# Gated linear attention with two feed-forward layers on one core: the second attention product in four column groups, and the second layer's weights prepared in two slots of three

## The chip, the core and the metric

The kernel runs on one core of a Trainium2 chip. The metric is the device time of one execution in microseconds. The core has a matrix engine (PE, with its weight loads shown apart as PEld), three elementwise engines (DVE, ACT, POOL) and a queue engine (SP) that issues most DMAs. They run side by side and wait for one another through semaphores.

## What is computed

A gated recurrence (an mLSTM cell) over 768 steps, 4 batches and 8 heads of width 40, and then two feed-forward layers over the 3072 tokens of width 320, each with 2048 hidden channels. All of it is in float32:

```
for t in range(S):
    m_new = max(f[t] + m, i[t]);  f_s = exp(f[t] + m - m_new);  i_s = exp(i[t] - m_new);  m = m_new
    C = f_s * C + i_s * outer(v[t], k[t]);   n = f_s * n + i_s * k[t]
    y[t] = sigmoid(o[t]) * (C @ q[t]) / max(|n . q[t]|, 1)
x = y as (3072, 320)
x = (h * clip(h + 3, 0, 6) / 6) @ w1_out     with h = x @ w1_in
x = (max(h, 0) ** 2) @ w2_out                with h = x @ w2_in
```

## The kernel before

**Attention.** The recurrence is cut into 12 chunks of 64 steps. A unit `u` is one chunk of one batch (48 units), all 8 heads together. For a unit, `at_S` (lines 355 to 382) makes the scores, `at_P` multiplies them with the decay weights `W` into the tile `Xm` (104 partitions, for each head 104 columns: 64 for the outputs of the chunk's steps, 40 for the next state), and **`at_Y`** (lines 398 to 408) makes the second product. For each head it multiplies `Xm`, as the stationary operand, with `Z` (104 partitions, 41 columns: the chunk's values, a column of ones, and the carried state). The first 64 columns of `Xm` give 64 rows of output at partitions 0 to 63 (line 404), the other 40 give the next state at partitions 64 to 103 (line 406). The output is 64 and 40 columns of the array, so the two products of a head sit in two column groups of it. Afterwards `at_C` copies the state into the next `Z`, and `at_n1` to `at_n3` normalise and gate the output.

A float32 product is one instruction in the program and two records in the trace, each a weight load and a matmul. So a unit's `at_Y` is 16 instructions, 16 records on line 404 and 16 on line 406.

**Feed-forward layers.** They are cut into slots `s` (200 of them; layer 1 is slots 0 to 103, layer 2 slots 104 to 199). A full slot has the first product of 128 hidden channels for 512 tokens (`mm_A`, line 551, 8 matmuls of 512 columns), the activation on ACT and DVE (`act1` line 560 or 562, `act1b` line 567 or 570), the split of the result into a high and a low part (`act2` line 575 on ACT, `act2b` line 580 on DVE), and two slots later the second product (`mm_B`, line 590, 12 matmuls of 320 columns). Every fp32 operand of the layers is taken apart into a high part in the faster fp32r format and a remainder. `t_pe`, `t_hi` and `t_lo` (lines 525 to 539) transpose and split the layer's input.

**Weights.** Each layer has 16 weight tiles, `wi` (first product, even `i`) and `wo` (second product, odd `i`). They arrive as 64-bit words. `w_load` fetches a tile, `w_exp` (line 486, ACT) mends the exponent, `w_b1` and `w_b2` (lines 492 and 498, DVE) put the float32 together in the tile `wt`, `w_hi` (line 507, ACT) and `w_lo` (line 512, POOL) make the two parts. Tile `i` of layer 2 stands in the place of tile `i` of layer 1. The tile `wi` with index `i` is first used by `mm_A` of slot 104 + i, `wo` with index `i` by the `mm_B` that runs in slot 105 + i.

**Order.** The first part of the program (to about 196 us) follows a list written out by hand, `FIRST`. From there on the order comes from the function `moe`: for each slot `mm_A`, `act1`, `act1b`, then the steps hooked to the slot's "pe" place, then `mm_B` of two slots ago, the steps hooked to its "ew" place, `act2` and `act2b`. A unit's `at_Y` is hooked to every second slot (`2 * u - 10`), `at_S` of the next unit right after it in the same slot. The steps on layer 2's weights are hooked from slot `s1 = 90` on.

Of the kernel before, what the change touches and what calls it, by code (L numbers as in the profile page):

```python
# [25 lines left out]
L = 64  # L26
# [78 lines left out]
def kernel(ctx, tc, qk, kn, va, gates, og, w1i, w1o, w2i, w2o, out):  # L105
    nc = tc.nc
# [7 lines left out]
    E0 = 64  # L114
    KX = E0 + D
# [32 lines left out]
    Z = [[const.tile([KX, H, DV], F32, name=f"Z{b}{i}") for i in range(2)] for b in range(B)]  # L148
# [249 lines left out]
    def at_Y(u):  # L398
        b, c = units[u]
        Xm = T["X", u]  # L400
        pool, tag = (ps_acc, "acc0") if u in (1, 3) else (ps_y, "y")
        Yp = pool.tile([KX, H, DV], F32, tag=tag, name="Yp")
        for h in range(H):
            nc.tensor.matmul(  # L404
                out=Yp[0:L, h, :], lhsT=Xm[:, h, 0:L], rhs=Z[b][c % 2][:, h, :], start=True, stop=True)
            nc.tensor.matmul(  # L406
                out=Yp[E0:KX, h, :], lhsT=Xm[:, h, L:KX], rhs=Z[b][c % 2][:, h, :], start=True, stop=True)
        T["Y", u] = Yp

    def at_C(u):  # L410
# [216 lines left out]
    w_bits = (w_b1, w_b2)  # L627
    w_hilo = (w_hi, w_lo)
# [11 lines left out]
    def at(s, part, f, *a):  # L640
        hooks.setdefault((s, part), []).append((f, *a))
# [31 lines left out]
    for u in range(6, NU):  # L673
        b, c = units[u]
        if c % 2:
            at(at_slot[u] + 3, "pe", x_T, 0, c // 2, b)
    for u in range(UL, NU):
        s = at_slot[u]
        if u >= 6:
            at(max(s - 6, 0), "ew", at_load, u)  # L680
            at(max(s - 6, 0), "ew", at_gload, u)
        if u >= 5:
            at(max(s - 4, 0), "ew", at_weights, u)
            at(max(s - 3, 0), "ew", at_x2, u)
        if u >= US:
            at(s - 3, "ew", qk_split, u)
        at(max(s - 2, 0), "pe", at_S, u)
        at(max(s - 2, 0), "ew", at_P, u)
        at(s, "pe", at_Y, u)
        at(s, "ew", at_C, u)  # L690
        at(s, "ew", at_norm, u)
    for j in range(NB):
        for i in range(B):
            at(first[1, j, 0] - 13 + 3 * i, "pe", x_T, 1, j, i)
    s1 = first[0, NB - 1, 0] + 2
    for i in range(NS):
        at(s1 + i, "ew", w_load, 1, i)
        at(s1 + i + 3, "ew", w_exp, 1, i)
        at(s1 + i + 4, "ew", w_bits, 1, i)
        at(s1 + i + 5, "ew", w_hilo, 1, i)  # L700
    for p, s in ((4, 45), (5, 45)):
        at(s - 6, "ew", o_load, p)
        at(s, "ew", o_sig, p)
# [3 lines left out]
        o_load, load_gates, o_sig, at_load, const_init, gate_m, gate_g, gate_G, gate_b,  # L707
        gate_bT, at_gload, w_load, w_add, w_mask, w_e, x_q, at_S, at_P, w_exp, x_k,
        w_b1, w_b2, at_Y, at_n1, at_n2, at_n3, at_C, w_hi, w_lo, warm, t_pe, t_hi,
        t_lo, mm_A, act1, act1b, act2, act2b, mm_B, evac)}  # L710
    todo = []
# [65 lines left out]
```

## Time and profile before

| | us |
|---|---|
| median of 3 runs | 871.29 (871.28 to 873.6) |
| the profiled execution | 871.86 |
| span of its instructions | 870.1 |
| PE busy in the span | 825.9 (95%) |
| DVE / ACT / POOL busy | 559.5 / 427.4 / 260.7 |

Read it in stretches, for the limits differ. Matmuls are pipelined and their ends are modelled, so the starts of records say more than their durations. A record with `x8` is a run of eight that follow each other; its first start is shown. The granted PE clock is full (2.4 GHz) from 119 us on; before that it falls to half in three short stretches.

### The profile page before, as it was taken

What the parts mean: (1) busy time and instruction counts of PE and PEld (TensorE: products, weight loads), DVE (VectorE), ACT (ScalarE), POOL (GpSimd) and SP (SyncE); (2) the same over time, 40 slices, a digit from 0 to 9 for tenths busy, and PEclk for the clock granted to TensorE, in tenths of its full rate; (3) what the DMA queues carried; (4) which work ended last, traced back from release to release, by engine and by line L of the source; (5) the groups of instructions that cost most, each with busy time, mean ns of one, the idle gap of its engine ahead of it and who ended that gap; (6) DMA issues with size and microseconds to landing.
All of it is one profiled execution on the core that took longest, in us unless ns stands there. A gap on an engine that the chain in (4) does not pass through costs nothing.

```text
span 870.1 us, 15963 instructions
## 1 busy us (share of the span) xinstructions
PE 825.9 (95%) x6288; PEld 738.0 (85%) x6288; DVE 559.5 (64%) x938; ACT 427.4 (49%) x817; POOL 260.7 (30%) x240
## 2 busy tenths in 40 slices
PE   3597999999999999999999999999999999999998
PEld 2486887888888888888889988999999999999997
DVE  4879889777878877777644999444444344444332
ACT  4656665645557455554434765343343433433433
POOL 4857865354454544545100444000000000000000
PEclk9999889999999999999999999999999999999999
DMA  8974521343633434333004540000000000000000
GB/s 222 269 232 134 169 81 36 92 100 96 170 92 97 103 86 108 95 81 82 1 3 167 201 163 1 1 31 1 1 31 1 20 12 1 31 1 1 31 1 31
DMA packets 30694, 66.82 MB, mean 77 GB/s; under 512 B 5116, under 2 KB 17468, under 8 KB 30620
## 3 DMA queue, kind: packets, MB, share of 16 engines
q1 hardware_dynamic: 30620, 65.82, 26.5%
q8 instruction: 49, 0.80, 0.4%
q14 instruction: 25, 0.20, 0.1%
HBM read 61.77 MB, written 4.03 MB: 76 GB/s over the span
## 4 chain that ended last, share of the span: by engine, by line
PE 73%; DVE 16%; issue 5%; ACT 3%; POOL 1%; DMA 1%; SPq 0%; DVEq 0%; POOLq 0%; ACTq 0%
PE hps L551 33%; PE acc L590 32%; DVE wt L492 4%; DVE gl L580 3%; PE Yp L404 3%; PE Sp L372 2%; DVE g L567 2%; PE tp L525 2%; DVE wt L498 1%; DVE X L444 1%; ACT yt L431 1%; ACT g L560 1%; DVE gh L575 1%; DVE Xm L395 1%; PE Sp L379 1%
## 5 line engine op out<-in xcount | busy, mean ns | idle before, releaser
L551 PE MATMUL hps<-xs,wi 128*128 128x512 f32 (+1 forms) x1600 | 392.6, 389 | 4.2 <-DVE g L567 2.4
L590 PE MATMUL acc<-wo,gh 128*128 128x320 f32 x1536 | 349.5, 314 | 0.3 <-ACT X L597 0.3
L551 PEld LDWEIGHTS hps<-xs,wi 128*128 128x128 f32 x1600 | 290.5, 193 | 53.5 <-DVE g L567 2.7
L590 PEld LDWEIGHTS acc<-wo,gh 128*128 128x128 f32 x1536 | 259.6, 189 | 9.9 <-ACT X L597 0.5
L590 PE MATMUL acc<-wo,gl 128*128 128x320 f32 x768 | 239.3, 312 | 5.0 <-DVE gl L580 5.0
L580 DVE TENSOR_TENSOR gl<-g,gh 128x512 fp32r<-128x512 f32 (+1 forms) x200 | 154.2, 771 | 61.7 <-ACT gh L575 60.6
L575 ACT CAST gh<-g 128x512 fp32r<-128x512 f32 (+1 forms) x192 | 115.1, 600 | 75.3 <-DVE g L570 58.7
L570 DVE TENSOR_TENSOR g<-g 128x512 f32<-128x512 f32 x96 | 66.4, 692 | 133.2 <-ACT g L562 133.2
L590 PEld LDWEIGHTS acc<-wo,gl 128*128 128x128 f32 x768 | 144.9, 189 | 7.6 <-DVE gl L580 7.5
L560 ACT ACTIVATE g<-hps,three 128x512 f32<-128x512 f32 (+1 forms) x104 | 67.8, 655 | 152.0 <-PE hps L551 138.4
L562 ACT ACTIVATE g<-hps 128x512 f32<-128x512 f32 x96 | 57.3, 597 | 143.4 <-PE hps L551 143.4
L567 DVE SCALAR_TENSOR_TENSOR g<-g,hps 128x512 f32<-128x512 f32 (+1 forms) x104 | 66.8, 644 | 65.0 <-ACT g L560 64.5
L329 POOL TENSOR_TENSOR Xm<-qkt,W 40x512 f32<-40x512 f32 x36 | 49.8, 1384 | 119.2 <-ACT W L319 113.6
L404 PEld LDWEIGHTS Yp<-Z,Xm 104*64 104x64 f32 x768 | 54.5, 151 | 21.8 <-issue 13.3
L404 PE MATMUL Yp<-Z,Xm 104*64 104x41 f32 x768 | 60.6, 244 | 8.8 <-DVE Xm L388 3.8
L300 POOL TENSOR_TENSOR W<-W,bT 104x512 f32<-104x512 f32 x43 | 59.4, 1382 | 3.4 <-DMA W<-Gd 3.0
L406 PE MATMUL Yp<-Z,Xm 104*40 104x41 f32 x768 | 52.7, 225 | 0.3 <-POOL Xm L340 0.3
L512 POOL TENSOR_TENSOR wi<-wt,wi 128x768 fp32r<-128x768 f32 x14 | 27.6, 1970 | 83.7 <-ACT wi L507 83.5
L340 POOL TENSOR_TENSOR Xm<-kI,W 104x320 f32<-104x320 f32 x43 | 40.5, 944 | 25.2 <-DMA Z<-in_va 10.4
L406 PEld LDWEIGHTS Yp<-Z,Xm 104*40 104x40 f32 x768 | 46.5, 123 | 0.4 <-POOL Xm L340 0.4
L351 DVE SCALAR_TENSOR_TENSOR qs<-qs,less,qkt 120x512 fp32r<-120x512 f32 x52 | 37.6, 764 | 7.5 <-ACT qs L349 7.3
L306 POOL TENSOR_SCALAR_AFFINE_SELECT W<-W 64x512 f32<-64x512 f32 x48 | 36.7, 767 | 9.7 <-DVE W L300 6.8
(90 smaller groups left out, 664.2 us busy)
## 6 DMA issues: line engine op xcount, KB each, us to landing
qkt<-in_qk SPq DMA_DIRECT2D x74, 160.0 KB
W<-Gd SPq DMA_DIRECT2D x48, 208.0 KB
rwi<-in_w1i SPq DMA_DIRECT2D x8, 768.0 KB
rwi<-in_w2i SPq DMA_DIRECT2D x8, 768.0 KB
rwo<-in_w1o SPq DMA_DIRECT2D x8, 640.0 KB
rwo<-in_w2o SPq DMA_DIRECT2D x8, 640.0 KB
Z<-in_va SPq DMA_DIRECT2D x48, 82.0 KB
X<-in_og SPq DMA_DIRECT2D x6, 640.0 KB
```

The costliest lines, as they stand in the source:

```text
L300: on("w_add", "g", u).tensor_tensor(out=W, in0=W, in1=bT[:, c, b * H:(b + 1) * H].unsqueeze(2).to_broadcast([KX, H, L]), op=ALU.add)
L329: on("x_q", "g", u).tensor_tensor(out=x_tile(u)[E0:KX, :, 0:L], in0=T["qk", u][E0:KX, 0], in1=T["W", u][E0:KX], op=ALU.mult)
L404: nc.tensor.matmul(out=Yp[0:L, h, :], lhsT=Xm[:, h, 0:L], rhs=Z[b][c % 2][:, h, :], start=True, stop=True)
L406: nc.tensor.matmul(out=Yp[E0:KX, h, :], lhsT=Xm[:, h, L:KX], rhs=Z[b][c % 2][:, h, :], start=True, stop=True)
L551: nc.tensor.matmul(out=h, lhsT=w[:, hl, kk, o:o + P], rhs=t[:, xk, i0 * P:i1 * P], start=(i == 0), stop=(i == len(TERMS) - 1))
L560: nc.scalar.activation(out=g, in_=T["h", s], func=ACTF.Relu, bias=three)
L562: nc.scalar.activation(out=g, in_=T["h", s], func=ACTF.Relu)
L567: nc.vector.scalar_tensor_tensor(out=g, in0=g, scalar=6.0, in1=T["h", s], op0=ALU.min, op1=ALU.mult)
L570: nc.vector.tensor_tensor(out=g, in0=g, in1=g, op=ALU.mult)
L575: copy("act2", s)(out=gh, in_=g)
L580: nc.vector.tensor_tensor(out=gl, in0=g, in1=gh.bitcast(F32), op=ALU.subtract)
L590: nc.tensor.matmul(out=acc[i], lhsT=g[:, n], rhs=w[:, hl, m % MG, :], start=(m == 0 and q == 0), stop=(m == NM - 1 and q == 2))
```

## The change

Two things. In `at_Y` each head's 104 columns of `Xm` are cut at 32, 64 and 96, so that four products (32, 32, 32 and 8 columns) stand where two (64 and 40) stood. The operands `Z`, the outputs and the waits are the same; a unit has 32 instructions and 64 records where it had 16 and 32. And the steps on layer 2's weights, one tile in every slot, are spread: `3 * i // 2` takes the place of `i`, so two tiles are treated in three slots. The loads keep their slots.

```diff
         for h in range(H):
-            nc.tensor.matmul(
-                out=Yp[0:L, h, :], lhsT=Xm[:, h, 0:L], rhs=Z[b][c % 2][:, h, :], start=True, stop=True)
-            nc.tensor.matmul(
-                out=Yp[E0:KX, h, :], lhsT=Xm[:, h, L:KX], rhs=Z[b][c % 2][:, h, :], start=True, stop=True)
+            for o in range(0, KX, 32):
+                e = min(o + 32, KX)
+                nc.tensor.matmul(
+                    out=Yp[o:e, h, :], lhsT=Xm[:, h, o:e], rhs=Z[b][c % 2][:, h, :],
+                    start=True, stop=True)
...
     for i in range(NS):
         at(s1 + i, "ew", w_load, 1, i)
-        at(s1 + i + 3, "ew", w_exp, 1, i)
-        at(s1 + i + 4, "ew", w_bits, 1, i)
-        at(s1 + i + 5, "ew", w_hilo, 1, i)
+        s = s1 + 3 + 3 * i // 2
+        at(s, "ew", w_exp, 1, i)
+        at(s + 1, "ew", w_bits, 1, i)
+        at(s + 2, "ew", w_hilo, 1, i)
```

The order of PE's instructions around the last unit's `at_Y`. `Yp` is the output, `Xm` and `Z` the operands, the shape is columns of `Xm` by columns of `Z`. Before:

```order
L551 MATMUL hps<-xs,wi_1421 128x512 x8
L404 MATMUL Yp<-Z_108,Xm 64x41
L406 MATMUL Yp<-Z_108,Xm 40x41
L404 MATMUL Yp<-Z_108,Xm 64x41
L406 MATMUL Yp<-Z_108,Xm 40x41
```

Now (line 406 is the one matmul of the new loop):

```order
L552 MATMUL hps<-xs,wi_1613 128x512 x8
L406 MATMUL Yp<-Z_108,Xm 32x41 x3
L406 MATMUL Yp<-Z_108,Xm 8x41
L406 MATMUL Yp<-Z_108,Xm 32x41 x3
L406 MATMUL Yp<-Z_108,Xm 8x41
```

Nothing else moved on PE: each head has four instructions in a row where it had two.

The order of DVE's instructions early in layer 2, where `wt` is the weight being put together, `g` and `gl` are the slot's activation and its low part. Before:

```order
L492 TENSOR_SCALAR wt<-rwi_6093 128x768
L498 SCALAR_TENSOR_TENSOR wt<-rwi_6093,wt 128x768
L580 TENSOR_TENSOR gl<-g,gh 128x512
L570 TENSOR_TENSOR g<-g 128x512
L492 TENSOR_SCALAR wt<-rwo_6130 128x640
L498 SCALAR_TENSOR_TENSOR wt<-rwo_6130,wt 128x640
L580 TENSOR_TENSOR gl<-g,gh 128x512
L570 TENSOR_TENSOR g<-g 128x512
L492 TENSOR_SCALAR wt<-rwi_6167 128x768
L498 SCALAR_TENSOR_TENSOR wt<-rwi_6167,wt 128x768
```

Now (the same steps have line numbers one higher):

```order
L493 TENSOR_SCALAR wt<-rwo_6736 128x640
L499 SCALAR_TENSOR_TENSOR wt<-rwo_6736,wt 128x640
L581 TENSOR_TENSOR gl<-g,gh 128x512
L571 TENSOR_TENSOR g<-g 128x512
L581 TENSOR_TENSOR gl<-g,gh 128x512
L571 TENSOR_TENSOR g<-g 128x512
L493 TENSOR_SCALAR wt<-rwi_6772 128x768
L499 SCALAR_TENSOR_TENSOR wt<-rwi_6772,wt 128x768
```

One slot in three now has no weight between its `g` and its `gl`.

## Rows read from the trace of the kernel before

**Rows 1.** Stretches: us, busy (count) of PE, PEld, DVE, ACT, POOL, clock, DMA.

```profile
0.00:118.00 118.00, 81.99 (x997) 72.74 (x998) 92.21 (x156) 71.04 (x179) 80.73 (x88) 0.93 0.66 194
...
196.00:440.00 244.00, 243.42 (x2185) 215.38 (x2184) 188.19 (x348) 128.87 (x211) 109.54 (x99) 1.00 0.36 90
...
515.00:540.00 25.00, 24.27 (x132) 20.81 (x132) 24.67 (x29) 16.53 (x30) 11.77 (x7) 1.00 0.08 27
```

**Rows 2.** The chain that ended last, shares by line, 196 to 440 us.

```profile
by line: PE hps L551 38.4%; PE acc L590 37.1%; PE Yp L404 9.4%; PE Sp L372 6.0%; PE tp L525 2.0%; PE Yp L406 1.4%; issue 1.2%; DVE qs L351 0.9%; ACT X L451 0.8%; DVE gl L580 0.6%; ACT L451 0.5%; ACT qs L349 0.4%; DVE g L567 0.4%; DVE Xm L39
```

**Rows 3.** The same chain from 138 to 197 us.

```profile
by line: PE acc L590 25.6%; PE hps L551 20.7%; DVE gl L580 9.0%; PE Yp L404 6.3%; DVE gh L575 5.5%; issue 5.2%; ACT g L560 4.5%; PE Sp L379 4.3%; DVE g L567 3.4%; ACT L319 2.2%; DVE Xm L395 2.2%; ACT X L451 2.0%; ACT W L319 2.0%; ACT X L597
```

**Rows 4.** Timeline of PE's matmuls in one slot: start, us, line, operation, shapes.

```profile
297.19 2.00 PE L551 MATMUL hps<-xs,wi 128*128 128x512 f32 x8
299.12 0.25 PE L404 MATMUL Yp<-Z,Xm 104*64 104x41 f32 x1
299.12 0.27 PE L406 MATMUL Yp<-Z,Xm 104*40 104x41 f32 x2
...
299.23 0.20 PE L406 MATMUL Yp<-Z,Xm 104*40 104x41 f32 x1
...
299.27 0.24 PE L406 MATMUL Yp<-Z,Xm 104*40 104x41 f32 x2
...
299.35 0.20 PE L406 MATMUL Yp<-Z,Xm 104*40 104x41 f32 x1
...
299.38 0.23 PE L406 MATMUL Yp<-Z,Xm 104*40 104x41 f32 x1
...
299.90 0.21 PE L406 MATMUL Yp<-Z,Xm 104*40 104x41 f32 x1
299.95 0.29 PE L404 MATMUL Yp<-Z,Xm 104*64 104x41 f32 x2
300.17 0.65 PE L372 MATMUL Sp<-qs 120*64 120x64 f32 x8
```

**Rows 5.** Line 404 from 196 to 440 us: count, ns min/median/max, first and last start.

```profile
L404 PE MATMUL Yp<-Z,Xm x432: 230/230/251, 198.1 to 436.3; 104*64 104x41 f32 x144
```

**Rows 6.** Timeline of PE at a block that started with an empty queue.

```profile
141.88 0.68 PE L379 MATMUL Sp<-qkt 40*64 40x64 f32 x16 [0.45 <-issue]
```

**Rows 7.** Line 404 from 141.7 to 142.3 us: the semaphore wait ahead of its block.

```profile
L404 PEldq EVENT_SEMAPHORE  x1: 51/51/51, 142.0 to 142.0; - x1
```

**Rows 8.** Timeline of PE: first products of slots without attention (85, 86, 87).

```profile
438.36 2.00 PE L551 MATMUL hps<-xs,wi 128*128 128x512 f32 x8
...
442.29 2.00 PE L551 MATMUL hps<-xs,wi 128*128 128x512 f32 x8
445.89 2.00 PE L551 MATMUL hps<-xs,wi 128*128 128x512 f32 x8
```

**Rows 9.** Timeline of PE: first products of slots 106 and 112.

```profile
515.86 2.00 PE L551 MATMUL hps<-xs,wi 128*128 128x512 f32 x8
...
540.20 2.00 PE L551 MATMUL hps<-xs,wi 128*128 128x512 f32 x8
```

**Rows 10.** Waits of PE's loads, 505 to 545 us: total us, times, longest.

```profile
PEld acc L590 <- DVE gl L580: 1.9, 5, 0.5
```

**Rows 11.** Groups by line, 505 to 545 us: count, busy us, mean ns, idle before.

```profile
L580 DVE TENSOR_TENSOR gl<-g,gh 128x512 fp32r<-128x512 f32 x12 | 8.7, 728 | 1.4 <-ACT gh L575 1.4
L512 POOL TENSOR_TENSOR wi<-wt,wi 128x768 fp32r<-128x768 f32 x4 | 7.8, 1945 | 9.4 <-ACT wi L507 9.4
L492 DVE TENSOR_SCALAR wt<-rwo 128x640 int32<-128x640 int32 x4 | 7.7, 1935 | 0.0
...
L570 DVE TENSOR_TENSOR g<-g 128x512 f32<-128x512 f32 x9 | 6.2, 685 | 0.0
...
L498 DVE SCALAR_TENSOR_TENSOR wt<-rwi,wt 128x768 int32<-128x768 int32 x4 | 3.8, 960 | 0.1
...
L536 DVE TENSOR_TENSOR xs<-tp,xs 128x256 fp32r<-128x256 f32 x2 | 0.8, 422 | 0.0
```

## The prediction

> **What bounds the kernel now.** I read the stretches first. From 196 to 440 us PE is busy for 243.4 of 244 us at the full clock, while DVE has 188 and POOL 110 [rows 1]: whatever PE is spared there comes off the end, as long as nothing else fills up. Before 118 us PE has 82 of 118 us, DVE 92, POOL 81: a mixture of waits, where a shorter PE block is mostly swallowed. From 515 to 540 us it is the other way round, DVE is busy for 24.67 of 25 us and PE waits. After that PE is gapless to the end. The chain of waits says the same: from 196 to 440 us it lies on PE, and lines 404 and 406, the second attention product, have 10.8% of it, 26 us [rows 2].
>
> Next the block itself [rows 4]. Read starts, not durations. The first product's last matmul starts shortly before 299, the block starts at 299.12 and the next block (line 372) at 300.17: 1.05 us, of which the 16 records of line 404 take 299.12 to 300.01, a record every 58 to 59 ns. Line 406 starts at the same 299.12, so the two column groups work at the same time. In its first records it goes faster: from 299.23 to 299.38, over 299.27, 299.31 and 299.35, four steps of 38 ns. Then it is held back to the pace of line 404 and ends at 299.90, only some 0.1 us ahead of it. So two things can be seen: a 64-column record costs 58 ns and a 40-column record 38 ns with the same 41 moving columns; and a later instruction may overtake waiting ones of the other group, but only by a few records, since line 406 never gets further ahead than that.
>
> **The second product in four groups.** It removes nothing of the arithmetic; it cuts the 64-column record, the slow one, into two of 32. Per group there are still 16 records one after the other (8 heads, two records each). At 58 ns these take 16 x 0.058 = 0.93 us; at the 38 ns of the 40-column records 16 x 0.038 = 0.61 us. 32 and 8 columns are fewer than 40, but the 41 moving columns are still there, so I take no less than 38 ns. The most that a unit can gain is thus 0.93 - 0.61 = 0.32 us.
>
> From this comes off what four groups need and two did not. First, overtaking: for the fourth group's record to start beside the first, it must pass one waiting record of each of the three other groups, three records, about as far as line 406 ran ahead of line 404. That is just enough for all four to run, with some loss; I charge 5 to 10% of 0.61 us, 0.05 us. Second, feeding: 32 instructions must reach the array in 0.6 us. The nearest row is a block that began with an empty queue [rows 6]: its eight float32 products started at 141.88, and PE's sequencer was at the wait that stands behind all eight by 142.0 [rows 7]. The rounding leaves 0.1 to 0.2 us, at most 25 ns an instruction, 0.8 us for 32 in the worst case and some 0.5 us in the best; but during the 1.9 us of matmuls of 512 columns ahead of the block the queue has time to fill, so part of the 32 is there at the start. I charge 0.02 us. The result is a gain of 0.25 us a unit, between 0.10 (groups half in step) and 0.32.
>
> How often does it count? Line 404 has 432 records from 196 to 440 us, 16 a unit, 27 units [rows 5]: 27 x 0.25 = 6.8 us (2.7 to 8.6). What is late next there is POOL, then DVE: 110 and 188 us of 244, which is no bound at 237 either. Of the 21 units before, the chain from 138 to 197 us has 6.3% of 59 us on line 404, 3.7 us, four units [rows 3]; between them it runs over DVE and ACT, so I count 0.8 us of their 1.0. Ahead of 138 us I count nothing, and 0.5 us of either sign for the order in which waits end there and for the half-clock stretches of that part.
>
> The trace shows a record every 29 ns over both groups (32 in 0.92 us). The Trainium skill (page "TensorEngine Tiling", section Instruction Overhead) speaks against the change: a matmul costs about 60 cycles however few columns it moves, so one should not take the tiling factor from a dimension that is already small. At the granted 2.4 GHz that is 25 ns; if it held for the whole array, 64 records would take an estimated 1.6 us, 0.7 us more than now. The two records that start together at 299.12 agree with it at most within one group.
>
> **The weights in two slots of three.** A slot without attention takes 442.29 to 445.89, 3.60 us, and 3.93 us (438.36 to 442.29) where the layer's input is transposed [rows 8]. The six slots 106 to 111 take 515.86 to 540.20, 24.34 us [rows 9]; two of them transpose, so they should take 4 x 3.60 + 2 x 3.93 = 22.26. The loss is 2.1 us, and PE's own waits agree: 1.9 us in five waits for `gl`, DVE's line 580 [rows 10]. The cause is DVE's sum. A slot with a weight has 0.73 (line 580) + 0.69 (line 570) + 1.94 (line 492) + about 0.9 (line 498) = 4.2 us [rows 11] against 3.60 on PE; the excess adds up from slot to slot until the two slots of lag are used up.
>
> Now three slots hold two weights: 3 x 1.42 + 2 x 2.84 = 9.9 us, and 0.8 us at most for a transposed block (two subtractions of up to 0.42 [rows 11]), 10.7, against 2 x 3.60 + 3.93 = 11.1 on PE. DVE falls behind by 0.6 us in the first weighted slot and, where that one is followed by a weight and a transpose, by 1.7 us in all, and catches up in the slot without a weight. Before, the excess of about 0.6 us a slot had to run for many slots before PE felt it, so I take the whole 2.1 us as gained (1.6 to 2.2). PE's matmuls after it follow without a gap, so it reaches the end.
>
> What the spread costs is time to the deadline. The last `wi` (index 14) has its DVE steps in slot 115 and its split in slot 116, and slot 118 needs it. ACT and POOL take 0.8 and 1.95 us for the split (POOL's piece is line 512 [rows 11], ACT's is the shorter one), so it is there at about the middle of slot 117, some 1.9 us early. The last `wo` (index 15), split in slot 117, is needed in slot 120. If that cover were gone it would cost one wait of up to 2 us, once. The steps are only moved later past other work on ACT and POOL, which have room there: 16.5 and 11.8 of 25 us [rows 1]. The loads keep their place on the queue.
>
> **Sum.** 871.86 (the profiled execution) - 6.8 - 0.8 - 2.1 = 862.2; it lies 0.57 above the median of the runs, so against that 871.3 - 9.7 = **861.6**.
>
> **Rivals.**
> A. The forecast: all four groups run together.
> B. Overtaking stops short: three groups run, the fourth waits for most of its records, and each unit gains at most 0.1 us. For it: line 406 was held back after a few records [rows 4]. Against it: three records ahead is just what is needed. Time: 871.3 - 2.1 - (0 to 2.7) - 0.3 = 866 to 869, say 867.5.
> C. The moving columns share one path. Four groups read the same 41 columns of `Z` four times. Line 551 moves 8 x 512 columns in at most 1.93 us (297.19 to 299.12), 2.1 columns per ns; the block at 141.88 moves 16 x 64 in 0.68 us less the last record's tail of some 0.2, 2.2 per ns [rows 4, 6]. I see no higher rate. Two groups of 41 stay below it, four would need 164 columns in 38 ns, twice that. If 2.2 is the limit, a round of four records takes 75 ns, a block 16 x 0.075 = 1.19 us, 0.27 us more than now: 27 x 0.27 = 7.3, less 2.1, so **876.5**. It decides as soon as a round takes over 58 ns. Against it: nothing in the rows shows the path full with small matmuls, the loads of 64 columns set the same pace in that block. The Trainium skill's page "TensorE: Matmul & The Clock Gate" (Measured speedup against the span model) has three column groups of 512 moving columns 2.38 times as fast as one, which no run here shows.
> D. A price per record for the whole array, whatever its group. The densest stretch is 23 to 29 ns a record [rows 4]. 64 records at 25 to 29 ns take 1.6 to 1.86 us, 0.7 to 0.9 more: 27 x 0.8 = 22, less 2.1, so about 891. Against it: the pairs at 299.12, and that line 404 goes on at 58 ns whether or not line 406 runs beside it.
>
> **Chances.** A 0.66, B 0.15, C 0.12, D 0.07. The spread of the weights gains its 2 us in all four. A change under 0.3% (2.6 us) is about what a measurement of this kernel cannot tell from none. A is faster; of B a little more than half; C and D are slower. Faster 0.75, same 0.06, slower 0.19. The range covers A to its ends (27 x 0.32 = 8.6, with 1.3 before 196 us, 2.2 and 0.5: 858.7) and B to its upper end, 869.3, and leaves C and D out.
>
> **What would show it.** In the new trace the block of the second product (from 196 to 440 us) should take 0.8 us to the next block instead of 1.05, with records of the four groups starting within some 20 ns of each other and a record per group every 38 to 43 ns; slots with attention should be 0.25 us shorter and the others as they were. Slots 106 to 111 should be 3.60 and 3.93 us long, without a wait of line 590 for `gl`. A round of 75 ns speaks for C; starts spaced evenly by 25 ns for D; one group trailing the other three for B. The forecast is wrong if the blocks get no shorter, or if DVE or POOL take over the stretch from 196 to 440 us.

## The result, and the profile after

| | median, us | range, runs | ratio to the kernel before | 95% interval |
|---|---|---|---|---|
| before | 872.44 | 871.28 to 874.01, 4 | | |
| changed | 860.34 | 858.38 to 861.24, 4 | 0.9857 | 0.9829 to 0.9885 |
| changed, once more (e10) | 860.09 | 857.02 to 862.32, 5 | 0.9863 | 0.9841 to 0.9884 |

The change saves 11.6 to 12.1 us; 9.7 were forecast. The profiled execution of the changed kernel is the fastest of its first four (858.38 us, span 856.6), so the two traces differ by 13.5 us, more than the medians.

Stretches of the changed kernel, to be read against [rows 1] (us, busy and count of PE, PEld, DVE, ACT, POOL, clock, DMA):

```profile
0.00:118.00 118.00, 77.11 (x1434) 67.74 (x1434) 94.51 (x157) 71.54 (x181) 82.55 (x88) 0.94 0.66 194
196.00:440.00 244.00, 241.83 (x3027) 213.19 (x3026) 185.96 (x351) 130.82 (x214) 109.91 (x98) 1.00 0.34 88
515.00:540.00 25.00, 25.00 (x143) 22.54 (x142) 20.05 (x28) 15.61 (x26) 9.09 (x5) 1.00 0.00 1
```

PE is no longer quite full from 196 to 440 us (2.2 us free where it had 0.6), DVE and POOL are where they were, and from 515 to 540 us PE is full and DVE has 5 us to spare where it had 0.3. The chain of waits in the second stretch has 6.0% on the second product where it had 10.8 [rows 2], and small shares for `qs` that were not there in that size:

```profile
by line: PE hps L552 35.4%; PE acc L591 34.4%; PE Yp L406 6.0%; PE Sp L372 5.3%; issue 2.9%; PE tp L526 2.2%; DVE qs L351 2.2%; ACT qs L349 2.1%; DMA Z<-in_va 1.4%; ACT X L598 1.3%; DMA kI<-in_kn 1.0%; ACT g L561 0.8%; ACT X L452 0.8%; SPq 
```

One slot, the timeline of PE's matmuls (start, us, line, operation, shapes) beside [rows 4]. The second line is an answer for the first 80 ns of the block alone:

```profile
290.33 2.00 PE L552 MATMUL hps<-xs,wi 128*128 128x512 f32 x8
...
292.26 0.28 PE L406 MATMUL Yp<-Z,Xm 104*32 104x41 f32 x8
...
292.26 0.80 PE L406 MATMUL Yp<-Z,Xm 104*32 104x41 f32 x64
292.99 0.65 PE L372 MATMUL Sp<-qs 120*64 120x64 f32 x8
```

From the block's start to the next block it is 0.73 us; it was 1.05. Eight records, two of each group, have started within 80 ns: all four groups run together. The group of all records in this block gives first and last start, 292.3 and 292.9. In finer figures of the same trace the four groups start 7 ns apart, a round of four takes 38 ns, and the last record starts 0.605 us after the first.

Where the 13.5 us of this pair of traces lie is read from the starts of slots. Slots 32, 85, 106 and 112 after:

```profile
191.91 2.00 PE L552 MATMUL hps<-xs,wi 128*128 128x512 f32 x8
...
426.99 2.01 PE L552 MATMUL hps<-xs,wi 128*128 128x512 f32 x8
...
504.49 2.00 PE L552 MATMUL hps<-xs,wi 128*128 128x512 f32 x8
...
526.73 2.00 PE L552 MATMUL hps<-xs,wi 128*128 128x512 f32 x8
```

Before, slot 32 started here (for the others see [rows 8, 9]; slot 85 is 438.36):

```profile
196.14 2.00 PE L551 MATMUL hps<-xs,wi 128*128 128x512 f32 x8
```

So 4.23 us were gained ahead of slot 32, 7.14 in slots 32 to 84, nothing up to slot 106, 2.10 in slots 106 to 111, and nothing more to the end (870.1 - 856.6 = 13.5). From slot 32 on all of these repeat to within 0.25 us in every trace below that has that part of the change (e8 changes slots 42 to 74 further); the first does not.

### The profile page after: what moved, and what is told of

The parts are those of the page before. It is cut to its first block, busy times and chain, and to the rows that moved or that the text cites. A ratio compares the mean times of both kernels' runs of the same rounds, so it can differ in the third digit from the quotient of the medians.

```text
span 856.6 us, 19035 instructions
## 1 busy us (share of the span) xinstructions
PE 804.5 (94%) x7824; PEld 717.7 (84%) x7824; DVE 549.3 (64%) x938; ACT 427.2 (50%) x817; POOL 263.2 (31%) x240
## 4 chain that ended last, share of the span: by engine, by line
PE 78%; DVE 9%; issue 4%; ACT 4%; POOL 3%; DMA 1%; SPq 1%; POOLq 0%; ACTq 0%; DVEq 0%
PE hps L552 37%; PE acc L591 35%; PE Yp L406 2%; DVE gl L581 2%; PE tp L526 2%; PE Sp L372 2%; DVE wt L499 1%; DVE g L568 1%; DVE wt L493 1%; ACT g L561 1%; POOL Xm L329 1%; DVE qs L351 1%; ACT qs L349 1%; DVE X L445 1%; POOL W L306 1%
## 5 line engine op out<-in xcount | busy, mean ns | idle before, releaser
L406 PEld LDWEIGHTS Yp<-Z,Xm 104*32 104x32 f32 (+1 forms) x3072 | 35.9, 111 | 26.6 <-issue 16.8
L406 PE MATMUL Yp<-Z,Xm 104*32 104x41 f32 (+1 forms) x3072 | 42.5, 211 | 13.6 <-issue 5.8
L445 DVE TENSOR_TENSOR X<-X,yt 64x320 f32<-64x320 f32 x34 | 31.7, 932 | 1.1
L513 POOL TENSOR_TENSOR wo<-wt,wo 128x640 fp32r<-128x640 f32 x16 | 26.6, 1664 | 18.5 <-ACT wo L508 18.4
```

The costliest lines, as they stand in the source:

```text
L406: nc.tensor.matmul(out=Yp[o:e, h, :], lhsT=Xm[:, h, o:e], rhs=Z[b][c % 2][:, h, :], start=True, stop=True)
L513: on("w_lo", "g", ph, i).tensor_tensor(out=w[:, 1], in0=f, in1=w[:, 0].bitcast(F32), op=ALU.subtract)
```

## The experiments

**One part alone.** In e1 only the weights' steps are spread, in e2 only the groups are cut. In e3 the whole change is made, but units 0 to 20 keep two groups, in e11 only those units have four and nothing else is changed. e9, e10 and e12 are kernels that were there already (before, changed, e1), run again.

```
e3:   for o, e in CUT4 if u >= 21 else CUT2:
e11:  for o, e in CUT4 if u < 21 else CUT2:      (weights as before)
      CUT2 = ((0, 64), (64, 104))
      CUT4 = ((0, 32), (32, 64), (64, 96), (96, 104))
```

> The kernel before with only the spread of the weights. Theory: the whole 2.1 us lies in slots 106 to 111, which go from 24.34 to 22.2 us (3.60, or 3.93 with a transpose), everything else stays, so the time falls by 2.1 us, ratio 0.9976. Rival (the deadline): the later tiles make PE wait once or twice between slots 112 and 120, and less than 1 us is left. Rival (the two edits feed each other): alone it gains clearly less or more than 2.1 us.

> The kernel before with only the four column groups. Theory: blocks of 0.73 us instead of 1.06 to the next block, so 23 of the 27 units from slot 32 on gain 0.32 us, three gain nothing and one loses 0.3 us (7.1 us), and the part before 196 us gains some 3 us: about 10 us, ratio 0.9885. The weights' loss in slots 106 to 111 stays at 2.1 us. If the part before 196 us gains only what was forecast (0.8 us), 7.9 us, ratio 0.991.

> The changed kernel, but units 0 to 20 keep two column groups; so up to about 186 us the program is the one of before. Theory 1 (shorter blocks of the first units gain some 3 us): this kernel lacks them and is 3 us slower than the changed one, 9.2 us faster than before, ratio 0.9895. Theory 2 (the gain before 196 us is scatter of the half-clock stretches, nothing to do with the blocks): as fast as the changed kernel, ratio 0.986.

| | median, us | beside it before | ratio | 95% interval |
|---|---|---|---|---|
| e1, weights | 868.35 | 872.25 | 0.9948 | 0.9931 to 0.9966 |
| e2, groups | 863.06 | 872.25 | 0.9892 | 0.9874 to 0.9909 |
| e3, groups from unit 21 on, weights | 859.93 | 872.25 | 0.9870 | 0.9850 to 0.9890 |

e2 gained 9.2 us, between the 10 of its theory and the 7.9 of the alternative, with 7.07 of them between slots 32 and 85 in its trace. The other two did not fit shorter blocks in the first units: e1 gained 3.9 us where its trace has 2.10 in slots 106 to 111, and e3 was as fast as the whole change (its theory 2) though it has two groups in the first part. Both said that the first 196 us scatter, or that something else shortens them. Four more kernels, with twelve runs of three of them, were made for that:

> The kernel before, unchanged, in the place of a changed kernel. In the kernel with the spread weights alone the time fell by 3.9 us, 1.8 more than the trace shows in slots 106 to 111, though its first 196 us are instruction for instruction those of before. Theory 1 (the runs that stand for the kernel before have a slower first part by their place in the series): this one is some 1.5 to 2 us faster than the kernel before, ratio 0.998. Theory 2 (scatter from run to run, or something in how a program lies on the chip): ratio 1.000 within its interval.

> The changed kernel, unchanged, beside the kernel before on the same chip. Steady part and weights by the traces: 7.07 + 2.10 = 9.2 us. Theory 1 (four groups gain nothing before 196 us): 9.2 us less than the kernel before in the same place of the series. Theory 2 (they gain some 3 us there): 12 us less than it.

> The kernel before with four column groups in units 0 to 20 alone; from slot 32 on and in the weights it is the kernel before. Theory 1 (the shorter blocks of the first units give the changed kernel its extra 2 to 3 us before 196 us): 2 to 3 us faster than before, ratio 0.997. Theory 2 (they give the forecast 0.8 us or nothing, and the rest comes from elsewhere): 0 to 0.8 us, ratio 0.999 to 1.000, as the first part of the kernels with two groups there scatters.

> The kernel with the spread weights alone once more, since it gained 3.9 us where its trace shows 2.1 in slots 106 to 111 and the first 440 us are those of before. Theory 1 (the first part really runs some 2 us shorter in this program, with the same instructions there): 3.9 us again, ratio 0.9955. Theory 2 (the first part scatters by several us from run to run, and six runs were luck): 2.1 us, ratio 0.9976.

| | median, us | beside it before | ratio | 95% interval |
|---|---|---|---|---|
| e9, before again | 872.12 | 871.66 | 0.9995 | 0.9982 to 1.0008 |
| e10, changed again | 860.09 | 871.66 | 0.9863 | 0.9841 to 0.9884 |
| e11, groups in units 0 to 20 | 869.35 | 871.86 | 0.9971 | 0.9956 to 0.9986 |
| e12, weights again | 870.23 | 871.86 | 0.9983 | 0.9972 to 0.9994 |

e9 shows no gain from its place in its series (the kernels timed together). e12, the same program as e1, gained 1.6 us: with 2.1 in the slots, the 1.8 us more of e1 did not come again (theory 2). e11 gained 2.5 us (theory 1), so shorter blocks of the first units seem to shorten the first part; e3, which lost nothing without them, stands against it.

All runs together say how firm this is. From slot 32's start on a kernel takes a fixed time (its trace gives it: 673.9 us before, 664.7 changed), so each timed span less that time is the start of slot 32 in that run. The 31 runs with four groups in the first units (changed, e2, e8 below, e10, e11) have 193.8 us in the mean, standard deviation 1.5; the 93 runs with two (before, e1, e3, e9, e12) 195.9, 1.5. The difference is 2.1 us, and if every run stood by itself its 95% bounds would be about 0.6. The means of the kernels say that the runs don't:

| start of slot 32, us | mean (runs) |
|---|---|
| four groups | changed 193.6 (4), e2 194.3 (5), e8 194.7 (5), e10 193.5 (5), e11 193.4 (12) |
| two groups | before 196.1 (58), e1 194.0 (6), e3 194.5 (5), e9 196.0 (12), e12 196.5 (12) |

e1 and e12 are one program and lie 2.5 us apart. e1, e2 and e3 ran in one series, and there two groups are as early as four, all three some 2 us ahead of the kernel before beside them (196.3, 11 runs). In the last series e11 is 3.1 us ahead of e12. With each of the ten means counted once the difference is 1.5 us, with 95% bounds of about 1.4. So a gain in the first part is likely, and its size is not settled. A single trace tells little of that size. These are slot 32 in e10, the same program as the changed kernel, and in e8, whose first part is also the same; the first profile had 191.91:

```profile
195.37 2.00 PE L552 MATMUL hps<-xs,wi 128*128 128x512 f32 x8
```

```profile
195.71 2.00 PE L552 MATMUL hps<-xs,wi 128*128 128x512 f32 x8
```

**The weights.** The trace of e12 in its slots 106 to 111, columns as in the stretches above, has the forecast 22.24 us, PE full, DVE with 17.55:

```profile
515.42:537.66 22.24, 22.24 (x128) 20.12 (x127) 17.55 (x25) 14.49 (x25) 7.07 (x4) 1.00 0.08 30
```

In e2, which has the weights as before, these slots take 24.34 us (505.67 to 530.01), as in [rows 9].

**Three groups.** If a record's price is set by its 41 moving columns, 32, 32 and 40 columns should do as well as four groups.

```
-            for o in range(0, KX, 32):
-                e = min(o + 32, KX)
+            for o, e in ((0, 32), (32, 64), (64, KX)):
```

> The changed kernel with three column groups of 32, 32 and 40 columns instead of four. Theory 1 (a record takes what its 41 moving columns or its 40 loaded ones need, 38 ns, whatever the number of groups): blocks of 0.61 us as with four, same time as the changed kernel, ratio 0.986. Theory 2 (each record costs something for the whole array, or the limited overtaking slows four groups): the block gets shorter than with four, 48 records instead of 64, and the kernel 1 us or more faster than the changed one. Theory 3 (with groups of at most 32 columns a record is faster than 38 ns by its load): the 40-column group sets the pace and the block is longer than with four.

977.53 us, ratio 1.1229 (1.1195 to 1.1262), 117 us more than the changed kernel. Theory 3 alone had a longer block, by the pace of the 40 columns; none had this size. PE in one of its blocks, first the whole, then its first records in three answers for 0.1 us each:

```profile
300.49 3.25 PE L405 MATMUL Yp<-Z,Xm 104*32 104x41 f32 x48
303.67 0.65 PE L372 MATMUL Sp<-qs 120*64 120x64 f32 x8
...
300.49 0.27 PE L405 MATMUL Yp<-Z,Xm 104*32 104x41 f32 x4
...
300.69 0.27 PE L405 MATMUL Yp<-Z,Xm 104*40 104x41 f32 x2
...
300.89 0.27 PE L405 MATMUL Yp<-Z,Xm 104*32 104x41 f32 x4
```

The block takes 3.18 us to the next. The four records of a head's two groups of 32 start at 300.49, its 40-column records at 300.69, the next head at 300.89: 0.20 us from one width to the other, 16 times 0.20 is 3.2. The 40 columns never run beside the 32, and each change of width takes 0.14 us from start to start where, in finer figures of this block, a group's second record follows after 0.05 (32 columns) or 0.06 (40). The profile of before had a sign of it: line 372, which is not cut into groups, started 0.16 us after the last record of line 404, which then ran at one every 0.058 [rows 4]. The Trainium skill says it outright (page "TensorEngine Tiling", section Key Properties): changing the tiling mode, not just the tile, drains TensorE. This trace agrees and gives the price, some 0.1 us a change.

The block alone would account for 48 x (3.18 - 0.73) = 118 us. That it comes so near is luck, two effects of some 20 us each cancel. From 196 us on 14 of the 27 units' slots are 8.5 to 9.0 us long instead of 7.4, together 19 us; in each of the 14, and in none of the other 13, the granted clock falls to its lower level (1.2 GHz) for a part. Both stretches below hold the end of a block; in the first the granted clock is full (2.4 GHz), in the second 0.86 in the mean, so part of it ran at the lower level. In the first part, on the other hand, the waits swallow some of the longer blocks: slot 32 starts at 224.8 us, 29 us later than in e10, where 21 longer blocks make 51.

```profile
240.00:252.00 12.00, 12.00 (x111) 10.01 (x110) 7.59 (x15) 5.30 (x9) 4.44 (x4) 1.00 0.27 76
252.00:264.00 12.00, 12.00 (x89) 10.41 (x87) 7.15 (x14) 4.09 (x7) 4.42 (x4) 0.86 0.62 182
```

**Order and width apart.** If changes of width are the cause, the same three groups with only one change a unit must be short. And the order of four groups tells how far a record can overtake.

```
e6:   for cut in (((0, 32), (32, 64)), ((64, KX),)):
          for h in range(H):
              for o, e in cut:
e5:   for o in range(0, KX, 32):
          e = min(o + 32, KX)
          for h in range(H):
```

> Three column groups of 32, 32 and 40 columns as in the kernel at 977.5 us, but first the groups of 32 of all heads, then the 40 columns of all heads. Theory (going from products of at most 32 columns to wider ones or back empties the array, some 0.14 us from start to start; there are 16 such changes in a unit with the heads in order, 1 here): a block takes 0.14 us for the change and 16 records each at about 40 and 59 ns, some 1.6 to 1.8 us to the next block instead of 3.18; from 196 to 440 us 27 x 1.5 = 40 us less than that kernel. Rival (the 40-column products can't run beside the others, however sorted, and each takes a price of its own): no shorter than 3.18 us.

> The changed kernel with the same 32 products of a unit in another order: all heads of group 0, then all heads of group 1, and so on. Theory (a record may pass only a few waiting ones of other groups): group 1's first record stands 14 or more behind the running one and can't pass, the groups run one after the other, a block takes about 64 x 38 ns = 2.4 us to the next block instead of 0.73, some 1.7 us x 27 = 46 us more from 196 to 440 us and up to as much per unit before. Rival (the four groups draw from the whole queue): blocks of 0.73 us as in the changed kernel, 860 us.

e6, one run, 879.87 us (beside it before 871.19); e5, one run, 903.42. A block of e6 (the second line is an answer for 0.1 us alone), and one of e5:

```profile
303.00 1.54 PE L406 MATMUL Yp<-Z,Xm 104*32 104x41 f32 x48
...
303.73 0.46 PE L406 MATMUL Yp<-Z,Xm 104*40 104x41 f32 x7
...
304.47 0.65 PE L372 MATMUL Sp<-qs 120*64 120x64 f32 x8
```

```profile
305.33 2.21 PE L406 MATMUL Yp<-Z,Xm 104*32 104x41 f32 x64
307.48 0.65 PE L372 MATMUL Sp<-qs 120*64 120x64 f32 x8
```

e6: 16 rounds of two 32-column records from 303.00 on, the 40-column records from 303.73 on, the next block at 304.47, together 1.47 us where the kernel with 16 changes had 3.18. Theory held, a little better than it said (a 40-column record takes 39 ns, not 59). So it is the change of width: with fifteen changes fewer the block is 1.71 us shorter, 0.11 us a change. With one change three groups are still 0.74 us a unit worse than four, for the 40 columns then run by themselves.

e5: 2.15 us, that is 64 records one after the other, mostly at 35 to 41 ns, with some overlap where one group ends and the next begins. The forecast was 2.4. In its trace the first record of a group starts beside the 13th of the 16 of the group before it, with three waiting records ahead of it; it does so at all three borders in the block. At the last border, records counted from 306.75 to 306.785 us, and then to 306.92:

```profile
L406 PE MATMUL Yp<-Z,Xm x8: 197/200/203, 306.6 to 306.8; 104*32 104x41 f32 x7, 104*8 104x41 f32 x1
L406 PE MATMUL Yp<-Z,Xm x14: 197/200/206, 306.6 to 306.9; 104*32 104x41 f32 x10, 104*8 104x41 f32 x4
```

When the first record of 8 columns has started, three of 32 are still to come. So a record passes three waiting ones of one other group, no more. It isn't three in all: e7 below has a record that passes eight, spread over three groups. Rival B hung on this number, and four groups head by head need only one of each group.

**What sets 38 ns.** e7 cuts the moving columns too.

```
+            for n in (slice(0, 21), slice(21, DV)):
                 for o in range(0, KX, 32):
                     ...
-                        out=Yp[o:e, h, :], ... rhs=Z[b][c % 2][:, h, :],
+                        out=Yp[o:e, h, n], ... rhs=Z[b][c % 2][:, h, n],
```

> The changed kernel with each of the 32 products of a unit cut in two along the moving columns (21 and 20 of 41): 128 records a unit, each group 32. Theory (a record in a group takes the longer of its load of 32 columns and its moving columns, at 1.2 columns a ns, and some 4 to 5 ns): 38 ns were set by the 41 moving columns; now the 32 loaded ones set 32 ns, a block takes 32 x 32 = 1.0 us, 1.15 to the next block. Rival 1 (38 ns is a fixed price of a record in a group): 32 x 38 = 1.22 us, 1.35. Rival 2 (the records of all groups share one issue, which was just hidden at 9.5 ns a record): 1.2 us or more with the starts spaced evenly.

884.24 us, one run. A block of it:

```profile
302.25 1.26 PE L407 MATMUL Yp<-Z,Xm 104*32 104x21 f32 x128
303.44 0.65 PE L372 MATMUL Sp<-qs 120*64 120x64 f32 x8
```

1.19 us to the next block; less the 0.12 us from the last record to line 372, 32 records a group in 1.07 us, 33 ns each, 8 ns over the four groups. Theory said 1.15 and 32, rival 1 1.35. So 38 ns was no fixed price: it came from the 41 moving columns. The 8-column group of e5, which runs mostly by itself, says the same: it too takes 38 ns a record in the mean. That with half the moving columns the 32 loaded ones are the longer shows at the start of e7's block, here its records up to 302.435 us:

```profile
L407 PE MATMUL Yp<-Z,Xm x23: 179/186/208, 302.3 to 302.4; 104*32 104x21 f32 x10, 104*32 104x20 f32 x6, 104*8 104x21 f32 x4, 104*8 104x20 f32 x3
```

The group of 8 columns has started seven records, the three groups of 32 only 16 of the 24 that stand ahead of the seventh. In finer figures its records follow each other after 25 to 27 ns there, those of 32 columns after 32; the same in every block from slot 32 on. Later all four groups keep in step at 33 ns. Whether the loads or the feeding of the instructions (64 in 1.07 us, 17 ns each) set the last nanosecond is not shown. But nothing that all groups share is full at 9.5 ns a record, which was rival 2.

**The four units that gained nothing.** In the trace of the changed kernel 23 of the 27 units gained 0.32 us each, those of slots 42, 58 and 74 only 0.01, and slot 48 became 0.31 longer. PE in slots 42 and 48 of the changed kernel:

```profile
236.19 2.00 PE L552 MATMUL hps<-xs,wi 128*128 128x512 f32 x8
238.12 0.81 PE L406 MATMUL Yp<-Z,Xm 104*32 104x41 f32 x64
239.36 0.62 PE L372 MATMUL Sp<-qs 120*64 120x64 f32 x8 [0.43 <-DVE qs L351]
...
262.42 2.00 PE L552 MATMUL hps<-xs,wi 128*128 128x512 f32 x8
264.35 0.80 PE L406 MATMUL Yp<-Z,Xm 104*32 104x41 f32 x64
265.99 0.62 PE L372 MATMUL Sp<-qs 120*64 120x64 f32 x8 [0.84 <-DVE qs L351]
```

The block is as short as elsewhere, but line 372 then waits for its operand `qs`: 1.24 us from block to block in slot 42 as before, 1.64 in slot 48. ACT casts `qs` (line 349, 1.04 us) behind four copies of the slot's sums (line 598, 1.55 us) in slots 41, 57 and 73, and slot 48 comes after a sigmoid with its table loads, which has put ACT behind in slot 46; two operations of DVE follow. ACT in the slot before slot 42:

```profile
235.28 1.55 ACT L598 ACTIVATE X<-acc 128x320 f32<-128x320 f32 x4
236.72 1.04 ACT L349 CAST qs<-qkt 120x1024 fp32r<-120x1024 f32 x1
```

```
-            at(s - 3, "ew", qk_split, u)
+            if u == 30:
+                at(s - 4, "pe", qk_split, u)
+            else:
+                at(s - 3, "pe" if u in (27, 35, 43) else "ew", qk_split, u)
```

> The changed kernel, but the preparation of the scores' operands (lines 349 and 351) of units 27, 35 and 43 stands ahead of the four copies of the slot's sums instead of behind them, and that of unit 30 a slot earlier. Theory (in slots 42, 58 and 74 the shorter block only made PE wait longer for this, and slot 48 gave 0.3 us back in the same way): slots 42, 58 and 74 go from 5.46 to about 5.0 us, slot 48 from 5.87 to 5.0 to 5.5, together 1.6 to 2.3 us less than the changed kernel, 858.4. Rival (ACT and DVE are full there and give it back in the neighbouring slots): slots 46 to 50 together as long as before, and less than 1 us gained.

859.78 us, beside before 871.19, ratio 0.9871 (0.9849 to 0.9892): by time no different from the changed kernel. By its trace slots 42, 58 and 74 fell from 5.46 to 5.00 us, as theory said; slot 48 from 5.87 to 5.48, but slot 49 rose from 4.19 to 4.88, as the rival said, with PE waiting behind DVE:

```profile
268.20 0.80 PE L406 MATMUL Yp<-Z,Xm 104*32 104x41 f32 x64 [0.42 <-DVE Xm L392]
...
274.00 0.55 PE L526 MATMUL tp<-ident,X 128*128 128x128 f32 x3 [0.73 <-DVE Xm L392]
```

From slot 41 to slot 85 it is 1.0 us ahead of the changed kernel. The first three moves are worth 1.35 us, the fourth costs 0.3. A median of five runs with this first part doesn't show that.

## Why the prediction was right, point by point

**The block.** Right, and a little better than said: 0.73 us to the next block where 0.8 was forecast. The 38 ns of the 40-column record in [rows 4] was the right price, for the right reason (e7). The 0.05 us charged for overtaking rested on three records in all; the limit is three of one group, and one of each is needed. The 0.02 us for feeding was small enough too, since e7 was fed an instruction every 17 ns and this block needs one every 19. What was lost is the start: the first two rounds take some 50 ns each, 0.03 us together, and line 372 follows the last record after 0.13 us instead of 0.16, which gives it back. So the gain was the whole 0.32 us of the upper bound, the last part of it by luck.

**27 units.** 6.8 us forecast, 7.1 measured, as two errors that nearly cancel: 23 units at 0.32 instead of 0.25 (+1.7 us), and four units that gained nothing or less (-1.3). The step that failed is the sentence on what is late next, POOL and DVE by their sums over 244 us. It was the queue of one slot: ACT's cast of `qs` behind other work, with DVE after it. That chain was in the profile of before, `qs` with 0.9% and 0.4% in [rows 2].

**The first part.** 0.8 us were forecast. All runs together have 2.1, and with each kernel's mean counted once 1.5 with bounds of about 1.4, so the term was probably too small, but 0.8 isn't excluded. The steady part and the weights, 8.9 us of the forecast, came to 9.2; what the kernel gained beyond that, 2.4 to 2.9 us, lies in this part. The place was wrong too. From slot 21 (140 to 144 us) to slot 32, where the forecast put its 0.8, the traces of the changed kernel, e2, e8, e10 and e11 have gained 0.05 to 0.6 us; whatever else was gained lies before slot 21, where nothing was counted. Which of the waits there it shortens isn't settled: one program's slot 32 scatters by up to 5 us from run to run (190.5 to 195.8 in e10), more than the gain.

**The weights.** 2.1 us forecast, 2.10 measured in every trace with the spread. No wait of line 591 for `gl` is left from 490 to 535 us, and no deadline was missed.

**Rivals.** B hung on overtaking, and there was more room than the prediction saw: three waiting records of one group can be passed (e5), eight over three groups (e7), and one of each group is needed. C is out: a round moves 4 x 41 columns in 38 ns, 4.3 columns a ns, twice the rate that [rows 4, 6] showed. D is out with 8 ns a record over the array in e7. The page's rule of about 60 cycles a matmul (the Trainium skill, "TensorEngine Tiling", Instruction Overhead), 25 ns at the granted 2.4 GHz, is not contradicted inside one group: the 8-column group of e7 took 25 to 27 ns a record at the start of the block. For the array it doesn't hold.

**What no rival had.** Had one of the cuts been wider than 32 columns, as in e4, a unit's block would have been 2.1 us longer than before instead of 0.3 shorter. The forecast took for granted that groups of any widths run together, since 64 and 40 did [rows 4]. Those two share one division of the array, as 32, 32, 32 and 8 share one; 32 and 40 don't. The forecast was right there without knowing why.

## What to carry to other kernels

Cut a product into column groups of one division of the array (all up to 32, or all up to 64 columns), interleave the groups head by head so that a record has at most three waiting ones of any one group to pass, and count a change of width as some 0.1 us. The gain of a shorter block ends where its successor's operand is made by another engine: look at the queue of that engine in the single slot, not at its sum over the stretch. Where the first part of a kernel scatters by more than the gain, take the gain of the steady part from the starts of slots, and for the first part many runs in more than one series; one program gained 3.9 us in six runs of one series (e1) and 1.6 in twelve of another (e12).

## What was not expected of the hardware

- Products of 32 and of 40 columns next to each other exclude each other: 0.14 us from start to start at each change, 0.05 or 0.06 within a width (e4); one change a unit instead of 16 takes 1.71 us off the block (e6).
- Four column groups start 7 ns apart and move 4.3 columns a ns together; with 20 or 21 moving columns a record starts every 8 ns over the array, and a group of 8 loaded columns can take 25 ns a record where one of 32 takes 32 (e7).
- A record of a column group passes three waiting records of one other group and no more (e5); over three groups it passed eight (e7).
- The same program reached slot 32 anywhere from 190.5 to 195.8 us (e10), while the rest took the same to within 0.1 us in both traces of that program.
